# Attention by four heads: key chunks of 128, two half chunks sharing the array by quarters, and one weight load moved ahead

## Chip, cores and metric

The kernel runs on one core of a Trainium2 chip. The metric is the device time of one execution in microseconds, the median of the runs shown. The profile is of one further execution.

## The reference, cut to what matters

Three stages follow one another. Batch 4, 12 heads, 448 positions, 64 columns for each head:

```python
scores = scale * np.matmul(q, k.transpose(0, 1, 3, 2)) - np.log(S)     # q, k, v: (4, 12, 448, 64)
attn = 1.0 / (1.0 + np.exp(-scores))
attn_out = np.matmul(attn, v)
x = attn_out.transpose(0, 2, 1, 3).reshape(1792, 768)
h = np.maximum(np.maximum(x @ w1, x @ w2), x @ w3)                     # w1, w2, w3: (768, 768)
x2 = h @ w_out                                                        # (768, 768)
g, val = x2 @ w_gate, x2 @ w_val                                      # (768, 1536) each
out = (g / (1.0 + np.exp(-g)) * val) @ wo2                            # (1536, 768)
```

The sigmoid has no sum over the keys, so the keys may be taken in any order and in chunks of any size. Keys and values must only be cut in the same way.

## The kernel before, in words

**Number format.** A product that needs near float32 accuracy is made of three matmuls in a faster 32-bit format (`PRODUCTS`): high part by high part, low by high, high by low. The pair of parts is made by `halves` or `split`: a cast, then a subtraction. The second attention product (probabilities by values) uses plain float32 operands, and the trace shows two matmul instructions for each of its `nc.tensor.matmul` calls.

**Attention.** Heads come in pairs: 24 of them, six for each batch. `load_pair` brings q, k and v of a pair in by nine DMAs on SP's queue: four for `rq`, four for `rk` (runs of 32 values) and one for `rv`. VectorE transposes q and k by blocks of 32 into `qT` and `kT`, where the first head lies on partitions 0 to 63 and the second on 64 to 127, and `halves` makes `qq` and `kk`. The 448 keys are cut into four chunks of 112. `score(c)` makes six matmuls, three products by two heads, with 64 rows of the array for each head; ScalarE turns the two banks of `ps` into probabilities `a` (L759). `attend(c0, c1)` multiplies two chunks at a time by the values, 64 columns of the array for each head, and adds into one bank. `close` copies that bank out as the two parts of `x`, or to DRAM (`dx`) for the rows that are worked on later.

**The order of the work.** Nothing is written out by hand. Each step is a task with a cost for each engine that may do it, what it reads and writes, and a due time. `Plan.order` lists the tasks against its own model of time, and among those that can start soon takes the one due first. The result is a fixed order of instructions for each engine, SP's queue included. Due times come from constants: `HEAD` and `PAIR` are the time of one pair in the first and the second half of attention, `T0` is when the first layer's products begin, `AHEAD0` to `AHEAD2` spread the early conversion of `w_gate` and `w_val` (`ahead`), of which the first `NEAR` of 24 units go through the first set of buffers (`raw`) and the others through a second (`raw2`, one load at a time).

**Stages.** First attention alone, for batches 0 and 1. From `T0` on the 36 products of the first layer for the first 768 rows (18 matmuls of 384 columns each, `m<-x,w`) are interleaved with attention of batches 2 and 3. Then `w_out` for those rows (`second_layer`). Then the first layer for the other 1024 rows in seven products instead of eight (`first_layer_1`, `stream`, `mult`): it needs left factors made from the weights by `seven` and right factors made from `dx` by `x_back` and `right`. Each product takes terms of all three right factors. `seven` and `x_back` both fetch through the two buffers `cc`, in the order in which the program adds them: `x_back` 0, 1 and 2 with two buffers each, and then `seven`. After that come `w_out` for these rows and the gated part.

**Buffers.** In PSUM: `m` three banks, `av` one, `ps` two times two banks, later `mm` in place of `ps`. The attention of batches 0 and 1 accumulates in `m`, the rest in `av`. `S`, which `seven` needs, belongs to a region (`rest`) that opens only when the first layer's input `x` is done with.

Of the kernel before, what the change touches and what calls it, by code (L numbers as in the profile page):

```python
# [62 lines left out]

HEAD = 6000.0
T0 = 78.0 * 1000.0
PAIR = 5900.0
EARLY = 9000.0
LAG = 4500.0


NEAR = 18
AHEAD0 = 78.0 * 1000.0
AHEAD1 = 270.0 * 1000.0
# [152 lines left out]
def t_mm(n):  # L226
    return 13.3 + n / 2.4


def sigmoid_attention_max_ffn_silu_ffn(tc, q, k, v, w1, w2, w3, wo, wg, wv, wo2, out):  # L230
# [27 lines left out]
    P = 128  # L258
# [6 lines left out]
    NO = DM // 2  # L265
    KC = 4
    C = S // KC
    PARTS = ((0, 768), (768, B * S))
# [42 lines left out]
    def turn(old, new):  # L311
# [85 lines left out]
    N1 = 3 * KF * 2  # L397
    STEP = p_mm(0) + NPAIR * (B - 2) * PAIR / N1
    T1 = T0 + N1 * STEP

    def pair_at(b, p):
        i = b * NPAIR + p
        if b < 2:
            return i * HEAD, i * HEAD + LAG
        t = T0 + (i - 2 * NPAIR) * N1 * STEP / (NPAIR * (B - 2)) - EARLY
        return t, t + 1.5 * LAG
# [147 lines left out]
    def seven(s, w, i, keep=True):  # L554
# [20 lines left out]
        cc = fetch_pair(d, d.pieces)  # L575
        sb = rest.buf("S", [P, 4, HC])
        s2, s3, s1, s4 = (sb.part() for _ in range(4))
# [34 lines left out]
    def rows_pair(s, i):  # L612

        out_ = []
        for j in range(2):
            wb = two.buf("wr", [P, 2, UC], F32R)
            if not s:
# [7 lines left out]
                continue  # L625
            rt, sb = half.buf("cc", [P, 2, UC]), rest.buf("S", [P, 4, HC])
            low, c = sb.part(), sb.part()
# [54 lines left out]

    def load_pair(b, h0):
# [7 lines left out]
        rv = att.buf("rv", [C, 2, KC, D])  # L691
# [22 lines left out]
    def pair(b, p):  # L714

        due_s, due_a = pair_at(b, p)
        step = (HEAD if b < 2 else PAIR) / KC  # L720
        rq, rk, rv = load_pair(b, 2 * p)
        half = [slice(0, D), slice(D, P)]

        def operand(key, raw, name):
# [7 lines left out]
            both = att.buf(name, [P, 2, S], F32R)  # L732
            return both, halves(t, both, slice(0, S), lambda: t.t, S, key=name)

        qq, q_b = operand("qT", rq, "qq")
        kk, k_b = operand("kT", rk, "kk")
        probs, pav = [], None

        def score(c):
# [12 lines left out]
            t = plan.add(  # L752
                {"pe": 100.0 + 3 * t_mm(S)}, run, reads=[*q_b, *k_b], writes=[psb], after=prev("s"),
                due=due_s + c * step,
            )
            in_turn("s", t)
            plan.add(
                {"act": t_act(2 * S)},
                lambda e: e.activation(ab.t[:C], psb.t[:C, :, :S], AF.Sigmoid, bias=bias[:C], scale=SCALE),  # L759
                reads=[psb], writes=[ab], after=prev("a"),  # L760
            )
            in_turn("a", ab.writers[-1])
            probs.append(ab)

        def attend(c0, c1):

            nonlocal pav
            if c0 == 0:
                pav = pm.buf("av" if b > 1 else "m", [P, 512])
# [8 lines left out]
            t = plan.add(  # L778
                {"pe": 150.0 + (c1 - c0) * 4 * S / 2.4}, run, reads=[rv, *probs[c0:c1]], writes=[pav],
                after=prev("av"), due=due_a + c0 * step,  # L780
            )
            in_turn("av", t)

        def close():

            n = min(max(PARTS[0][1] - b * S, 0), S)
            if n:
# [23 lines left out]

        return score, attend, close

    def attention(b):
        for p in range(NPAIR):
            score, attend, close = pair(b, p)
            for c in range(KC):
                score(c)
            for c in range(0, KC, 2):
                attend(c, c + 2)  # L820
            close()

# [231 lines left out]

    def first_layer_1(facs):
        plan.kind = "b"
        hs = [None] * KF
        for i in range(HD):
# [5 lines left out]
            for wi, w in enumerate((w1, w2, w3)):  # L1064
# [117 lines left out]
    plan.kind = "h"  # L1182
    for b in range(B):
        attention(b)
    turn([att, ps], [pmb, half])
# [17 lines left out]
    hs = first_layer_1(facs)  # L1203
    plan.kind = "w"
# [41 lines left out]
```

## Time and profile before

| what | value |
|---|---|
| median of three runs | 992.12 us (991.72 to 997.26) |
| the profiled execution: its own time, its span | 992.58 us, 990.5 us |
| TensorE busy | 972.7 us, 98% of the span |
| VectorE, ScalarE, GpSimd busy | 641.9, 440.3, 141.8 us |
| granted TensorE clock, mean | 0.993 |

The span runs from the first to the last instruction; the time outside it is 2.1 us. A busy TensorE counts pipelined matmuls, so 98% says that it hardly waits, not that it computes at its peak.

### The profile page before, as it was taken

To read this page: it belongs to the slowest core of one execution; us is meant where nothing else is said; L and a number is where in the kernel's file an instruction comes from. 1 tells how busy PE (TensorE), PEld (TensorE's weight loads), DVE (VectorE), ACT (ScalarE), POOL (GpSimd) and SP (SyncE) were. 2 spreads that over 40 slices of the span, in tenths; PEclk is the share of its full clock that TensorE was granted. 3 is DMA by queue.
4 is the path that set the end of the run, shared out by engine and by line. 5 is a ranking of instruction groups with operands and counts; after the bars stand their busy time and mean duration, and the time that the engine had idled before them with its cause. 6 is when DMAs were issued, how large, how long until landed. Compare 5 with 4: busy or idle time off the path is not lost.

```text
span 990.5 us, 13658 instructions
## 1 busy us (share of the span) xinstructions
PE 972.7 (98%) x5139; PEld 816.0 (82%) x5139; DVE 641.9 (65%) x972; ACT 440.3 (44%) x618; POOL 141.8 (14%) x113
## 2 busy tenths in 40 slices
PE   8999999999999799999999999999999999999998
PEld 4444777777799688888878989898898999999998
DVE  5664576666667787874678486958687743455545
ACT  5876577677765643322445451605154322111110
POOL 0101000000000112320002022325344400000000
PEclk9999999999999899999999999999999999999999
DMA  7888999999989651125237665748589874567542
GB/s 125 185 170 184 246 291 274 259 292 252 306 303 309 233 160 49 64 74 181 92 125 278 240 230 184 271 167 271 192 304 321 282 262 175 184 215 244 184 143 100
DMA packets 191202, 208.52 MB, mean 211 GB/s; under 512 B 116128, under 2 KB 166560, under 8 KB 191136
## 3 DMA queue, kind: packets, MB, share of 16 engines
q1 hardware_dynamic: 191136, 207.65, 66.7%
q8 instruction: 40, 0.66, 0.3%
q14 instruction: 26, 0.21, 0.1%
HBM read 132.91 MB, written 74.71 MB: 210 GB/s over the span
## 4 chain that ended last, share of the span: by engine, by line
PE 87%; DMA 5%; DVE 3%; ACT 2%; SPq 2%; issue 1%; DVEq 0%; ACTq 0%
PE m L867 45%; PE mm L867 20%; PE av L867 12%; PE ps L747 5%; PE av L774 4%; DMA wraw<-in_moe_w_dram 2%; SPq L698 2%; PE m L774 1%; DMA wraw<-in_moe_w_val_dram 1%; DMA rq<-in_q_dram 1%; ACT a L759 1%; DVE u L665 1%; DMA cc<-dh 1%; DVE o L1151 0%; DVE w L349 0%
## 5 line engine op out<-in xcount | busy, mean ns | idle before, releaser
L867 PE MATMUL m<-T,w 128*128 128x512 f32 (+1 forms) x1557 | 334.0, 369 | 1.0 <-DVE T L349 0.9
L867 PEld LDWEIGHTS m<-T,w 128*128 128x128 f32 x1557 | 284.2, 188 | 40.5 <-DVE T L349 2.0
L867 PE MATMUL mm<-wr,g 128*128 128x384 f32 x1008 | 177.1, 334 | 0.1
L867 PEld LDWEIGHTS mm<-wr,g 128*128 128x128 f32 x1008 | 175.1, 188 | 0.9 <-DVE o L1151 0.4
L1023 DVE TENSOR_TENSOR u<-m,u 128x512 f32<-128x512 f32 (+1 forms) x111 | 71.2, 644 | 92.6 <-PE m L867 90.8
L867 PEld LDWEIGHTS m<-x,w 128*128 128x128 f32 x648 | 110.8, 188 | 20.1 <-issue 12.1
L867 PE MATMUL av<-T,w 128*128 128x512 f32 (+1 forms) x522 | 119.8, 373 | 6.4 <-ACT w L346 5.9
L867 PE MATMUL m<-x,w 128*128 128x384 f32 x648 | 122.0, 340 | 0.0
L867 PEld LDWEIGHTS av<-T,w 128*128 128x128 f32 x522 | 96.5, 190 | 20.5 <-ACT w L346 6.2
L1151 DVE TENSOR_TENSOR o<-mm,o 128x768 f32<-128x768 f32 (+1 forms) x84 | 67.8, 821 | 57.6 <-PE mm L867 57.6
L759 ACT ACTIVATE a<-ps,bias 112x896 f32<-112x896 f32 x96 | 91.5, 1004 | 11.4 <-PE ps L747 11.1
L747 PE MATMUL ps<-qq,kk 64*112 64x448 f32 x576 | 73.9, 385 | 5.0 <-ACT a L759 3.6
L747 PEld LDWEIGHTS ps<-qq,kk 64*112 64x112 f32 x576 | 47.0, 175 | 37.8 <-ACT a L759 21.1
L445 ACT ACTIVATE r<-wraw 128x768 int32<-128x768 uint32 x48 | 43.6, 908 | 54.3 <-DMA wraw<-in_moe_w_dram 16.2
L349 POOL TENSOR_TENSOR g<-t,g 128x512 fp32r<-128x512 f32 (+1 forms) x21 | 28.0, 1332 | 249.3 <-ACT g L346 240.1
L466 DVE SCALAR_TENSOR_TENSOR c<-c,r 128x768 int32<-128x768 int32 x48 | 46.2, 962 | 21.0 <-ACT r L458 16.1
L458 ACT ACTIVATE r<-wraw 128x768 f16<-128x768 f32 x48 | 52.1, 1086 | 0.9
L346 ACT CAST w<-S 128x768 fp32r<-128x768 f32 x34 | 28.5, 837 | 50.8 <-PE m L867 33.1
L346 ACT CAST g<-t 128x384 fp32r<-128x384 f32 (+1 forms) x43 | 23.9, 560 | 56.9 <-DVE t L1092 52.2
L583 POOL TENSOR_TENSOR S<-cc 128x384 f32<-128x384 f32 x16 | 16.9, 1057 | 196.6 <-DVE w L349 135.8
L867 PE MATMUL mm<-h,w 128*128 128x384 f32 (+1 forms) x216 | 44.2, 362 | 0.0
L774 PE MATMUL m<-a,rv 112*64 112x448 f32 x192 | 43.1, 571 | 0.0
(105 smaller groups left out, 1010.4 us busy)
## 6 DMA issues: line engine op xcount, KB each, us to landing
ds_S<-w SPq DMA_DIRECT2D x24, 768.0 KB, 4.4
w<-ds_S SPq DMA_DIRECT2D x24, 768.0 KB, 5.4
dp<-c SPq DMA_DIRECT2D x42, 384.0 KB, 6.1
cc<-dp SPq DMA_DIRECT2D x21, 768.0 KB, 5.1
wraw<-in_moe_w_dram SPq DMA_DIRECT2D x18, 768.0 KB, 6.2
wraw<-in_moe_w_gate_dram SPq DMA_DIRECT2D x12, 768.0 KB, 6.7
wraw<-in_moe_w_val_dram SPq DMA_DIRECT2D x12, 768.0 KB, 6.2
ds_A<-w SPq DMA_DIRECT2D x12, 768.0 KB, 6.4
```

Of the source, the lines that this page charges most:

```text
L346: (eng.copy if eng is nc.scalar else eng.tensor_copy)(o, i)
L349: eng.tensor_tensor(out=o, in0=a, in1=b, op=ALU.subtract)
L445: lambda e: e.activation(rb_at(), word(0).bitcast(U32), AF.Copy, scale=0.875 * 2.0 ** -29, bias=0.4999),
L458: lambda e: e.activation(rb_at().bitcast(F16).rearrange("p (c two) -> p c two", two=2)[:, :, 1], word(1).bitcast(F32), AF.Copy, scale=2.0 ...
L466: lambda e: e.scalar_tensor_tensor(c_at().bitcast(I32), c_at().bitcast(I32), 3, rb_at(), ALU.logical_shift_left, ALU.bitwise_or),
L698: nc.sync.dma_start(out=r.t[D * j + 32 * e:D * j + 32 * e + 32], in_=src[b, h0 + j, :, 32 * e:32 * e + 32].rearrange("(c i) d -> i c d", i ...
L747: nc.tensor.matmul(psb.t[:C, j, :S], kk.t[half[j], wh, c * C:(c + 1) * C], qq.t[half[j], xh], start=(i == 0), stop=(i == 2),)
L759: lambda e: e.activation(ab.t[:C], psb.t[:C, :, :S], AF.Sigmoid, bias=bias[:C], scale=SCALE),
L774: nc.tensor.matmul(pav.t[half[j], :S], rv.t[:, j, c], probs[c].t[:C, j], start=(c == 0), stop=(c == KC - 1),)
L867: nc.tensor.matmul(acc.at(n), l(), r(), start=(i == 0), stop=(i == len(terms) - 1))
L1023: lambda e: e.tensor_tensor(out=o.t[:, :n], in0=acc.at(n), in1=x.t[:, :n], op=ALU.add),
L1151: lambda e, o=o, b=banks[0].b, nh=nh: e.tensor_tensor(out=o.t[:, nh], in0=b.t[:, nh, :NO], in1=o.t[:, nh], op=ALU.add),
```

## The change

Attention goes by quads, two pairs of heads at a time. Of the 448 keys 384 are taken as three chunks of 128, and chunk `c` is now every third key from `c` on (so that a partition of `rv` reads three keys in one run of 768 bytes). The last 64 keys of both pairs make one common chunk: pair `g` takes the columns of half `g` of the array and head `j` the rows of half `j`, so four matmuls of 64 by 64 in plain float32 use the four quarters, from `kT` and `qT` themselves; the four matmuls by the values use the quarters too. A quad has seven score steps where two pairs had eight. Two steps together still make one `attend` task, which may now reach from one quad into the next (`group`, `flush`). `rv` comes by two DMAs instead of one. Attention always accumulates in `av`, which has two banks now, and `m` has two instead of three; later products alternate between `m` and `av`. The attention rings are longer. The constants of due times are others, with `SPREAD` putting the second half's attention into the first 0.8 of the interleaved stage, and `NEAR` falls from 18 to 12. `S` moves to the region `half`, which opens earlier, and the first `seven` is added after two of the three `x_back`.

```diff
-HEAD = 6000.0
-T0 = 78.0 * 1000.0
-PAIR = 5900.0
+QUAD = 10600.0
+T0 = 71.0 * 1000.0
+SPREAD = 0.8
...
-NEAR = 18
-AHEAD0 = 78.0 * 1000.0
+NEAR = 12
+AHEAD0 = 71.0 * 1000.0
...
-    KC = 4
-    C = S // KC
+    CW = S // P
+    KW = CW * P
+    KC = CW + 1
...
-        "att", dict(rq=2, rk=2, rv=3, qT=2, kT=2, qq=2, kk=2, a=4, xf=2), side="right",
+        "att", dict(rq=2, rk=2, rv=4, qT=3, kT=3, qq=3, kk=3, a=5, xf=2), side="right",
     )
-    half = Region("half", {"cc": 2, "u": 4, **{f"T0{i}": 1 for i in range(7)}}, side="right")
-    rest = Region("rest", {"S": 1, **{f"T{kk}{i}": 1 for kk in range(1, HD) for i in range(7)}}, side="right")
+    half = Region("half", {"cc": 2, "u": 4, "S": 1, **{f"T0{i}": 1 for i in range(7)}}, side="right")
+    rest = Region("rest", {f"T{kk}{i}": 1 for kk in range(1, HD) for i in range(7)}, side="right")
...
-    pm = Region("pm", dict(m=3, av=1), space=PSUM)
+    pm = Region("pm", dict(m=2, av=2), space=PSUM)
...
-        t = T0 + (i - 2 * NPAIR) * N1 * STEP / (NPAIR * (B - 2)) - EARLY
+        t = T0 + (i - NPAIR) * SPREAD * N1 * STEP / NPAIR - EARLY
...
+
             nc.sync.dma_start(
-                out=rv.t.rearrange("p h c d -> p (h c) d"),
-                in_=v[b, h0:h0 + 2].rearrange("h (c p) d -> p (h c) d", p=C),
+                out=rv.t[:, :, :CW], in_=v[b, h0:h0 + 2, :KW].rearrange("h (p c) d -> p h c d", c=CW),
+            )
+            nc.sync.dma_start(
+                out=rv.t[side, :, CW], in_=v[b, h0:h0 + 2, KW:].rearrange("h p d -> p h d"),
             )
...
             def run(_):
+                if len(gs) > 1:
+                    for g in gs:
+                        (qt, *_), (kt, *_), _ = pairs[g]
+                        for j in range(2):
+                            nc.tensor.matmul(
+                                psb.t[half_p[g], j, :S], kt.t[half_p[j], cols], qt.t[half_p[j]], start=True, stop=True,
+                            )
+                    return
+                (_, qq, _), (_, kk, _), _ = pairs[gs[0]]
                 for i, (xh, wh) in enumerate(PRODUCTS):
                     for j in range(2):
                         nc.tensor.matmul(
-                            psb.t[:C, j, :S], kk.t[half[j], wh, c * C:(c + 1) * C], qq.t[half[j], xh],
+                            psb.t[:, j, :S], kk.t[half_p[j], wh, cols], qq.t[half_p[j], xh],
                             start=(i == 0), stop=(i == 2),
                         )
...
             def run(_):
-                for c in range(c0, c1):
+                for g in gs:
+                    at = half_p[g] if len(gs) > 1 else slice(0, P)
                     for j in range(2):
                         nc.tensor.matmul(
-                            pav.t[half[j], :S], rv.t[:, j, c], probs[c].t[:C, j], start=(c == 0), stop=(c == KC - 1),
+                            accs[g].t[half_p[j], :S], pairs[g][2].t[at, j, c], ab.t[at, j],
+                            start=first[g], stop=last[g],
                         )
...
+        A, X, Z = (0,), (0, 1), (1,)
+        n = 0
+        for gs, c, first, last in (
+            *((A, c, {0: c == 0}, {0: False}) for c in range(CW)),
+            (X, CW, {0: False, 1: True}, {0: True, 1: False}),
+            *((Z, c, {1: False}, {1: c == CW - 1}) for c in range(CW)),
+        ):
+            ab = score(n, gs, slice(KW, S) if gs == X else slice(c, KW, CW))
+            attend(n, gs, c, ab, first, last)
+            ends.extend(lambda g=g: close(g) for g in gs if last[g])
+            n += 1
+            if len(group) == 2:
+                flush()
+        return flush
...
-        return Acc(pm.buf("av" if "late" in chain and count % 4 == 3 else "m", [P, 512]))
+        return Acc(pm.buf("av" if "late" in chain and count % 2 else "m", [P, 512]))
...
-                left = seven(1, w, i, keep=False)
+                if i or wi:
+                    left = seven(1, w, i, keep=False)
...
-    facs = [x_back(i) for i in range(HD)]
+    facs = [x_back(i) for i in range(2)]
+    plan.kind = "w"
+    left = seven(1, w1, 0, keep=False)
+    plan.kind = "x"
+    facs += [x_back(i) for i in range(2, HD)]
```

## Rows read from the trace of the kernel before

**Rows 1.** The page: the chain that ended last, shares of the span by engine.

```profile
PE 87%; DMA 5%; DVE 3%; ACT 2%; SPq 2%; issue 1%; DVEq 0%; ACTq 0%
```

**Rows 2.** Windows by stage: busy us and instructions per engine, granted clock, DMA share, GB/s.

```profile
7.80:94.20 86.40, 82.65 (x513) 38.17 (x513) 53.30 (x97) 65.05 (x83) 8.88 (x6) 0.96 0.85 171
94.20:276.70 182.50, 182.47 (x1063) 137.10 (x1061) 115.38 (x183) 126.00 (x152) 4.00 (x3) 1.00 0.95 272
276.70:320.40 43.70, 43.70 (x252) 43.55 (x252) 33.01 (x52) 27.15 (x44) 0.00 (x0) 1.00 0.89 302
320.40:331.30 10.90, 4.49 (x11) 3.01 (x11) 7.85 (x13) 6.92 (x10) 0.38 (x1) 0.69 0.93 322
331.30:453.70 122.40, 122.40 (x541) 101.35 (x541) 96.33 (x136) 44.12 (x62) 28.68 (x25) 1.00 0.33 106
```

**Rows 3.** Timeline of TensorE in attention alone: start, length (us), line, count.

```profile
56.37 1.46 PE L747 MATMUL ps<-qq,kk 64*112 64x448 f32 x12
57.76 1.72 PE L774 MATMUL m<-a,rv 112*64 112x448 f32 x8
59.41 0.46 PE L747 MATMUL ps<-qq,kk 64*112 64x448 f32 x2
```

**Rows 4.** Score matmuls and weight loads, 56.2 to 59.5 us: shortest, median, longest (ns).

```profile
L747 PEld LDWEIGHTS ps<-qq,kk x14: 169/171/173, 56.4 to 59.4; 64*112 64x112 f32 x14
```

**Rows 5.** The chain in order of time: start, length (us), what.

```profile
110.31 3.33 PE m L867 x18
...
289.37 6.24 PE m L867 x36
...
331.29 6.12 PE m L867 x27
```

**Rows 6.** Groups by form: count, busy us, mean ns, idle before and its releasers.

```profile
L466 DVE SCALAR_TENSOR_TENSOR c<-c,r 128x768 int32<-128x768 int32 x48 | 46.2, 962 | 21.0 <-ACT r L458 16.1 <-ACT c L451 4.4
L452 DVE TENSOR_SCALAR c<-wraw 128x768 f32<-128x768 f32 x37 | 20.9, 564 | 30.8 <-DMA dp<-c 23.0 <-DMA wraw<-in_moe_w_dram 3.9 <-DMA wraw<-in_moe_w_out_dram 2.7
L346 DVE CAST w<-c 128x768 fp32r<-128x768 f32 x19 | 10.6, 557 | 0.4
```

**Rows 7.** Timeline of TensorE where the first layer's second part begins.

```profile
326.50 1.22 PE L867 MATMUL av<-T,w 128*128 128x512 f32 x2 [5.92 <-ACT w L346]
```

**Rows 8.** The fetches into `cc` on SP's queue there, and ScalarE's first split.

```profile
303.67 0.32 SPq L831 DMA_DIRECT2D cc<-dx  x1
...
311.42 0.32 SPq L831 DMA_DIRECT2D cc<-dx  x1
...
318.54 0.60 SPq L538 DMA_DIRECT2D cc<-dp  x1
...
325.61 0.83 ACT L346 CAST w<-cc 128x768 fp32r<-128x768 f32 x1 [0.37 <-DMA cc<-dp]
```

**Rows 9.** One fetch each, issued at 318.54, 4.30 and 4.84 us: KB, us to landing.

```profile
cc<-dp SPq DMA_DIRECT2D x1, 768.0 KB, 7.1
...
rk<-in_k_dram SPq DMA_DIRECT2D x1, 56.0 KB, 2.1
...
rv<-in_v_dram SPq DMA_DIRECT2D x1, 224.0 KB, 3.8
```

**Rows 10.** Timeline of SP's queue in attention alone: start, time of issue (us), count.

```profile
53.39 2.07 SPq L698 DMA_DIRECT2D rq<-in_q_dram  x4
...
71.42 0.49 SPq L706 DMA_DIRECT2D rv<-in_v_dram  x1
72.00 5.50 SPq L698 DMA_DIRECT2D rq<-in_q_dram  x4
```

**Rows 11.** Timeline, 72 to 80 us: the twelfth pair's last transpose and its scores.

```profile
72.25 0.65 DVE L728 STREAM_TRANSPOSE kT<-rk 128x448 f32<-128x448 f32 x1 [0.32 <-DMA rk<-in_k_dram]
...
74.71 1.50 PE L747 MATMUL ps<-qq,kk 64*112 64x448 f32 x12
...
79.74 1.76 PE L747 MATMUL ps<-qq,kk 64*112 64x448 f32 x12 [1.87 <-ACT a L759]
```

More of the change, by code (lines that the diff above doesn't have):

```diff
@@ L397, in sigmoid_attention_max_ffn_silu_ffn, with quad_at @@
     N1 = 3 * KF * 2
-    STEP = p_mm(0) + NPAIR * (B - 2) * PAIR / N1
+    STEP = p_mm(0) + NPAIR * (B - 2) * QUAD / 2 / N1
     T1 = T0 + N1 * STEP
-    def pair_at(b, p):
-        i = b * NPAIR + p
+    def quad_at(b, g):
+        i = b * (NPAIR // 2) + g
         if b < 2:
-            return i * HEAD, i * HEAD + LAG
-        t = T0 + (i - 2 * NPAIR) * N1 * STEP / (NPAIR * (B - 2)) - EARLY
+            return i * QUAD, i * QUAD + LAG
+        t = T0 + (i - NPAIR) * SPREAD * N1 * STEP / NPAIR - EARLY
         return t, t + 1.5 * LAG
@@ L575, in seven @@
         cc = fetch_pair(d, d.pieces)
-        sb = rest.buf("S", [P, 4, HC])
+        sb = half.buf("S", [P, 4, HC])
         s2, s3, s1, s4 = (sb.part() for _ in range(4))
@@ L625, in rows_pair @@
                 continue
-            rt, sb = half.buf("cc", [P, 2, UC]), rest.buf("S", [P, 4, HC])
+            rt, sb = half.buf("cc", [P, 2, UC]), half.buf("S", [P, 4, HC])
             low, c = sb.part(), sb.part()
@@ L681, in sigmoid_attention_max_ffn_silu_ffn, with load_pair @@
     dram_x = {}
-    def load_pair(b, h0):
+    def load_pair(b, h0, side):
         def fetch(dst, cost, run):
@@ L690, in load_pair @@
         rq, rk = (att.buf(key, [P, NB, 32]) for key in ("rq", "rk"))
-        rv = att.buf("rv", [C, 2, KC, D])
+        rv = att.buf("rv", [P, 2, KC, D])
         for src, r in ((q, rq), (k, rk)):
@@ L712, in load_pair, with quad @@
         return rq, rk, rv
[L714 to L722, printed above, removed]
+    half_p = [slice(0, D), slice(D, P)]
+    group = []
+    def quad(b, p0):
+        due_s, due_a = quad_at(b, p0 // 2)
+        step = QUAD / 7
         def operand(key, raw, name):
@@ L732, in operand, with score @@
             both = att.buf(name, [P, 2, S], F32R)
[L733 to L739, printed above, removed]
+            return t, both, halves(t, both, slice(0, S), lambda: t.t, S, key=name)
+        pairs = []
+        for g in range(2):
+            rq, rk, rv = load_pair(b, 2 * (p0 + g), half_p[g])
+            pairs.append((operand("qT", rq, "qq"), operand("kT", rk, "kk"), rv))
+        accs = [None, None]
+        def score(n, gs, cols):
             psb = ps.buf("ps", [P, 2, 512])
@@ L752, in score @@
             t = plan.add(
-                {"pe": 100.0 + 3 * t_mm(S)}, run, reads=[*q_b, *k_b], writes=[psb], after=prev("s"),
-                due=due_s + c * step,
+                {"pe": 100.0 + (3 * t_mm(S) if len(gs) == 1 else 4 * S / 2.4)}, run,
+                reads=[x for g in gs for y in pairs[g][:2] for x in (y[2] if len(gs) == 1 else y[:1])],
+                writes=[psb], after=prev("s"), due=due_s + n * step,
             )
@@ L758, in score @@
                 {"act": t_act(2 * S)},
-                lambda e: e.activation(ab.t[:C], psb.t[:C, :, :S], AF.Sigmoid, bias=bias[:C], scale=SCALE),
+                lambda e: e.activation(ab.t, psb.t[:, :, :S], AF.Sigmoid, bias=bias, scale=SCALE),
                 reads=[psb], writes=[ab], after=prev("a"),
@@ L762, in score, with attend, flush, close @@
             in_turn("a", ab.writers[-1])
[L763 to L769, printed above, removed]
+            return ab
+        def attend(n, gs, c, ab, first, last):
+            for g in gs:
+                if first[g]:
+                    accs[g] = pm.buf("av", [P, 512])
             def run(_):
-                for c in range(c0, c1):
+                for g in gs:
+                    at = half_p[g] if len(gs) > 1 else slice(0, P)
                     for j in range(2):
                         nc.tensor.matmul(
-                            pav.t[half[j], :S], rv.t[:, j, c], probs[c].t[:C, j], start=(c == 0), stop=(c == KC - 1),
-                        )
+                            accs[g].t[half_p[j], :S], pairs[g][2].t[at, j, c], ab.t[at, j],
+                            start=first[g], stop=last[g],
+                        )
+            group.append((run, [*(pairs[g][2] for g in gs), ab], [accs[g] for g in gs], due_a + n * step))
+        def flush():
+            todo, group[:] = list(group), []
             t = plan.add(
-                {"pe": 150.0 + (c1 - c0) * 4 * S / 2.4}, run, reads=[rv, *probs[c0:c1]], writes=[pav],
-                after=prev("av"), due=due_a + c0 * step,
+                {"pe": 150.0 + len(todo) * 4 * S / 2.4}, lambda e: [run(e) for run, *_ in todo],
+                reads=[x for _, r, _, _ in todo for x in r], writes=[x for _, _, w, _ in todo for x in w],
+                after=prev("av"), due=todo[0][3],
             )
             in_turn("av", t)
-        def close():
+            for f in ends:
+                f()
+            ends[:] = []
+        def close(g):
+            p, pav = p0 + g, accs[g]
             n = min(max(PARTS[0][1] - b * S, 0), S)
@@ L810, in close, with attention @@
             plan.add({"sp": 650.0}, store, reads=[xf], writes=[piece], tail=TAIL, due=due_a + 20000.0)
[L812 to L821, printed above, removed]
+        A, X, Z = (0,), (0, 1), (1,)
[12 more added lines that the diff above has]
+        return flush
+    ends = []
+    def attention():
+        for b in range(B):
+            for p0 in range(0, NPAIR, 2):
+                flush = quad(b, p0)
+        if group:
+            flush()
     def x_back(i):
@@ L1053, in stream, with first_layer_1 @@
         last(0, 1, mult("S4", "B22"), u[1])
-    def first_layer_1(facs):
+    def first_layer_1(facs, left):
         plan.kind = "b"
@@ L1182, in sigmoid_attention_max_ffn_silu_ffn @@
     plan.kind = "h"
-    for b in range(B):
-        attention(b)
+    attention()
     turn([att, ps], [pmb, half])
@@ L1202, in sigmoid_attention_max_ffn_silu_ffn @@
         ahead(w, f, False, AHEAD1 + (i + 1) * (AHEAD2 - AHEAD1) / (len(todo) - NEAR), raw2, AHEAD1)
-    hs = first_layer_1(facs)
+    hs = first_layer_1(facs, left)
     plan.kind = "w"
```

## The prediction

> **What bounds the kernel now.** I read the chain of waits first. It lies 87% on TensorE [rows 1], so a microsecond taken from TensorE counts unless something else becomes late, and only there. Then I cut the span into stages by windows [rows 2]. In attention alone, 7.8 to 94.2 us, TensorE is busy 82.65 of 86.40 us with a mean clock of 0.96. From there to 320.4 us it never rests. Then comes the one large hole, 320.4 to 331.3 us: 4.49 of 10.90 us busy and a mean clock of 0.69. The next stage is full again. So the change touches three places: attention alone, attention among products, and the hole.
>
> The reader should also see the transfers. The DMA share is 0.85, 0.95, 0.89 and 0.93 in the first four windows and 0.33 in the fifth [rows 2]. The loads are nearly as tight as TensorE as far as 331 us, and slack behind it.
>
> **Attention on TensorE.** A block is two chunks. Its twelve score matmuls start at 56.37 us, its eight value matmuls at 57.76, the next block at 59.41 [rows 3]: 1.39 + 1.65 = 3.04 us. Two chunks for 24 pairs are 48 blocks now. The change makes 12 quads of seven steps, 84 steps or 42 blocks: 6 x 3.04 = 18.2 us less, half of it in each half of attention. That chunks have 128 keys and not 112 adds nothing to a matmul that streams the same 448 columns.
>
> The common chunk costs some of it back. Its score is plain float32, in the two-instruction form of the value matmuls, where one chunk takes 1.65/2 = 0.83 us; an ordinary chunk's score takes 1.39/2 = 0.70: +0.13. It also changes how the array is divided, once more among the scores and once more among the values. What such a change costs I read from the products: 18 matmuls alone between others take 3.33 us, 36 in a row 6.24, so 3.12 for 18 [rows 5]: 0.21 each. So +0.13 + 2 x 0.21 = 0.55 for each quad, 6.6 us for 12. No row shows the array in four quarters. The bounds are no extra (18.2 us gained) and twice as many changes (another 5.0 us lost); I take the middle, since rows 3 show halves by rows and halves by columns each running their two matmuls together. Net: -18.2 + 6.6 = -11.6 us.
>
> [...]
>
> **Weights with a step.** The score's key columns now lie three elements apart. A weight load of 112 columns lasts 171 ns [rows 4], and its matmuls follow every 1.39/6 = 0.23 us; 128 columns would take 171 x 128/112 = 195 ns and stay hidden. The nearest rows for reading with a step are on VectorE: every second word of 768 takes 564 ns, a cast of 768 neighbours 557 [rows 6]. So I take zero; the other bound is a rival below.
>
> **Products of the first layer.** Before, almost each of the 36 stands between attention blocks and pays the 0.21. With attention pressed into 0.8 of the stage, the last seven or so follow one another: 7 x 0.21 = -1.5 us (bounds 0 and -3). Three banks of `m` become two. The cover is the next product: a bank is needed again over 3 us after it was filled, and an eviction takes about half a microsecond. Zero; if an eviction waits behind a conversion that itself waits for a load, it costs one wait at a time.
>
> **Loads in attention alone.** SP issues four DMAs for q in 2.07 us [rows 10], 0.52 each. A pair had nine and gets ten, 5.2 us instead of 4.7: over 12 pairs +6.2 us on a queue whose values of the twelfth pair went out at 71.42 us. [...] The values go in longer runs. At the start one `rk` DMA landed 2.1 us after its issue at 4.30 us and the `rv` behind it 3.8 us after 4.84, so `rv` took 8.64 - 6.40 = 2.2 us of the transfers [rows 9]; runs three times as long may save between 0 and 1.4 us of it, I take 0.6, 7 us for 12 pairs. So the queue's end moves little, perhaps 1.5 us earlier, while TensorE's work there shrinks by 6. Before, the twelfth pair's last transpose began at 72.25 us and its scores at 74.71 [rows 11], some 2.5 us of slack. 6 - 1.5 - 2.5 = 2 us of new waiting: +2 (bounds 0 and +5). Behind an SP that is late stand the first weights and the stores of `dx`; with `T0` at 71 they are not pressing. The wait of 1.87 us at 79.74 [rows 11], a probability step behind a conversion, can go or turn up elsewhere; I leave it, plus or minus 2.
>
> **The hole at 320 us.** Nine matmuls of 512 columns take 6.12/3 = 2.04 us [rows 5]. Here they took the window's 10.90, so 8.9 us were lost: 5.92 of standing still until ScalarE's split of a left factor [rows 7], and most of the rest in matmuls at the lower of the two clock levels after the rest. The split ran at 325.61 when the fetch landed; the fetch was issued at 318.54, behind `x_back`'s at 303.67 and 311.42 [rows 8], and took 7.1 us to land [rows 9]. The change gives `seven` the place of 303.67 or so, and moves the last two fetches of `x_back` back by one place each. The left factors then are early. But the second product needs a difference of both halves of the third right factor: if that fetch goes out at 318.5 and takes 7.1 us, it lands at 325.6, and the hole is only some 2 us shorter. [...] I take -5 (bounds 0 and -8.9).
>
> **Six units moved.** They go to where the DMA share is 0.33 and VectorE busy 96.33 of 122.40 us [rows 2]. Each adds 0.96 + 0.56 us on VectorE [rows 6], 9 us in all: 105 of 122. Covered, zero. Were VectorE late, the products would wait for banks.
>
> **Sum.** On the profiled execution, span 990.5: -11.6 - 1.5 + 2 - 5 = -16.1, so 974.4 us; with 2.1 outside the span 976.5. That execution lies 0.5 us above the median (992.58 against 992.12): **976.0 us**.
>
> **Rivals.**
> First: the hole stays, as a wait for the right factor instead of the left one, and the loads hold attention back in full. Then 5 and 3 us of the sum fail: 984. For it speaks that SP's queue and `cc` keep their two buffers and their order; against it, the lighter traffic.
>
> Second, the change doesn't do what it says: quarters of the array do not run four at a time but two. Then the common chunk takes double its 0.83 us in scores and again in values, 1.66 a quad, 20 us in 12: 996. For it: in the trace matmuls only ever run in twos. Against: both kinds of two are there, by rows and by columns.
>
> Third, slower than before: reading weights with a step of three slows their loads. It decides once a load lasts longer than the 0.23 us between matmuls. At half pace 195 becomes 390 ns, 0.16 more for each pair of matmuls; 12 quads x 6 chunks x 3 pairs = 216, so +35 us: 1011. For it: nothing in the trace reads with so wide a step. Against: VectorE's step of two, which costs 7 ns in 557. [...]
>
> **How the numbers follow.** Forecast, all terms inside their bounds: 0.58. First rival 0.22. Second 0.08. Third 0.07. Better than every middle value, near 960: 0.05. For the range I add the terms' bounds as independent misses: about 8 to 9 us either way from 976, and the first rival's 984 with the same again halved. 963 to 989 holds the forecast and most of the first rival, and leaves out the second, the third and the extreme. A change of about 1% is what this measurement can tell, the runs before lying between 991.72 and 997.26. Below 982.2 us lie the forecast but for its upper end (0.53), a third of the first rival (0.08) and the best case (0.05): faster 0.66. Above 1002.0 lies the third rival and a piece of the second: slower 0.09. Within 1%: 0.25.
>
> **What the profile after would show.** Blocks of 3.04 us seven for two quads, with the common chunk's four score matmuls of 64 by 64 starting together in 0.8 us; if they start in twos, the second rival. Score weight loads near 195 ns with matmuls 0.2 us apart; near 390 the third. The first value blocks of the last batches end earlier by some 6 us when `m<-x,w` begins and by 13 when it ends. In the hole, ScalarE's split ahead of the last product of `second_layer`, and TensorE waiting, if at all, for VectorE's `T` or `u`. VectorE no longer idle between 331 and 454 us but TensorE still full. The prediction is wrong if SP's queue, not TensorE, carries the chain before 80 us, or if the hole is as long as before.

## The result and the profile after

| | before | after |
|---|---|---|
| median, beside each other on one chip | 994.38 us (991.72 to 997.26, 4 runs) | 980.85 us (978.36 to 981.55, 4 runs) |
| ratio after to before | | 0.9859 [0.9819, 0.9899] |
| profiled execution, span | 992.58, 990.5 us | 978.36, 976.1 us |

The forecast was 976.0 us (963 to 989), with a span 16.1 us shorter; the span is 14.4 us shorter. The place of the gain is not quite the forecast one. The chain of waits of the kernel after, shares of the span:

```profile
PE 82%; DMA 7%; DVE 4%; SPq 3%; issue 2%; ACT 1%; DVEq 0%; ACTq 0%
```

TensorE's share falls from 87% [rows 1], and DMA with SP's queue rises from 7% to 10%: the chain now runs through loads somewhere. In the first 80 us TensorE has 8.1 + 5.5 + 2.2 = 15.8% of it (10.7 + 10.3 = 21.0% in the kernel before). The chain of the kernel after by line, from 0 to 80 us, as far as the view prints it:

```profile
by line: SPq L699 29.2%; DMA rk<-in_k_dram 18.5%; PE av L793 8.1%; issue 6.1%; DMA rq<-in_q_dram 5.9%; DVE kT L734 5.7%; PE ps L764 5.5%; DVE kk L347 3.3%; SPq L711 2.4%; DVE kk L350 2.4%; PE ps L757 2.2%; DVE x L350 1.8%; SPq L708 1.8%; DV
```

The windows say where TensorE loses time. After, columns as in [rows 2]:

```profile
50.80:60.10 9.30, 6.22 (x26) 1.97 (x24) 5.48 (x10) 4.81 (x6) 0.00 (x0) 0.63 0.71 132
53.90:60.04 6.14, 6.14 (x22) 1.90 (x22) 4.05 (x8) 3.28 (x4) 0.00 (x0) 0.52 0.71 131
315.40:331.30 15.90, 15.90 (x71) 13.13 (x71) 14.27 (x21) 9.75 (x15) 2.32 (x2) 1.00 0.89 300
331.30:443.90 112.60, 112.60 (x498) 93.23 (x498) 97.09 (x138) 51.96 (x71) 29.95 (x25) 1.00 0.53 173
```

One stretch in attention alone, 50.8 to 60.1 us, is bad: 3.08 us standing, and the 6.14 us behind it at a mean granted clock of 0.52: 0.50 in each microsecond from 53.9 to 58.9, and 1.00 again from 59.9. (The 0.63 of the whole window counts the standing too.) The lower clock costs 6.14 x 0.48 = 2.9, so the stretch loses 6.0 us. The hole of before (4.49 of 10.90 us busy at 0.69; the clock stood at 0.50 from 326.4 to 330.0 us) is gone: from 315.40 to 331.30 us TensorE is busy throughout and the clock is 1.00.

Two points of the chain split the gain. `w_out` for the first rows began before at

```profile
283.13 6.24 PE mm L867 x36
```

and the second product after it at 331.29 [rows 5]. After, the chain in order of time (start, length, what):

```profile
277.79 6.39 PE mm L910 x36
...
317.47 2.04 PE m L910 x9
```

| piece of the span | forecast | measured |
|---|---|---|
| until `w_out` begins (attention, products, loads) | -11.1 | 277.79 - 283.13 = -5.3 |
| from there to the second product of the next stage (the hole) | -5 | 39.68 - 48.16 = -8.5 |
| the rest | 0 | 658.6 - 659.2 = -0.6 |

So the first piece gave half of what was forecast and the hole gave more. Attention after, timeline of TensorE:

```profile
18.73 1.56 PE L764 MATMUL ps<-qq,kk 64*128 64x448 f32 x12
20.23 1.72 PE L793 MATMUL av<-a,rv 128*64 128x448 f32 x8
21.88 1.56 PE L764 MATMUL ps<-qq,kk 64*128 64x448 f32 x12
...
53.90 1.77 PE L757 MATMUL ps<-qT,kT 64*64 64x448 f32 x8 [3.08 <-ACT a L777]
...
61.54 1.89 PE L793 MATMUL av<-a,rv 64*64 64x448 f32 x12
63.35 1.56 PE L764 MATMUL ps<-qq,kk 64*128 64x448 f32 x12
...
66.50 0.95 PE L764 MATMUL ps<-qq,kk 64*128 64x448 f32 x6
67.38 0.98 PE L757 MATMUL ps<-qT,kT 64*64 64x448 f32 x8
68.29 1.72 PE L793 MATMUL av<-a,rv 128*64 128x448 f32 x8
...
245.91 31.88 PE L910 MATMUL m<-x,w 128*128 128x384 f32 x180
```

Read from start to start, an ordinary block is 1.50 + 1.65 = 3.15 us (3.04 before). The common chunk's eight score instructions take 68.29 - 67.38 = 0.91 us, about what an ordinary chunk takes: the four quarters run side by side. The pair of score chunks with the common one takes 68.29 - 66.50 = 1.79 against 1.50, its values 63.35 - 61.54 = 1.81 against 1.65: +0.45 us for each quad.

That holds where both pairs are ready. In three common chunks of attention alone the second pair's matmuls start only when the first pair's are through, and TensorE's rows count that as busy. Timeline of its weight loads, the second pair's in two of them; the first pair's start at 25.03 and 42.70:

```profile
25.93 0.20 PEld L757 LDWEIGHTS ps<-qT,kT 64*64 64x64 f32 x4 [0.71 <-DVE kT L734]
...
43.55 0.19 PEld L793 LDWEIGHTS av<-a,rv 64*64 64x64 f32 x4 [0.66 <-DVE x L350]
```

The one waited for the second pair's `kT`, the other for VectorE's copy out of the accumulator bank. With a third one, at 30.86 us, 0.90 + 0.85 + 1.06 = 2.8 us are lost so.

Who was late at 53.90? The row names a probability step `a`. VectorE and ScalarE just before it:

```profile
51.70 0.65 DVE L734 STREAM_TRANSPOSE qT<-rq 128x448 f32<-128x448 f32 x1 [1.90 <-DMA rq<-in_q_dram]
52.37 0.56 ACT L347 CAST qq<-qT 128x448 fp32r<-128x448 f32 x1 [4.96 <-DVE qT L734]
52.84 1.90 ACT L777 ACTIVATE a<-ps,bias 128x896 f32<-128x896 f32 x2
```

ScalarE's order has a cast of a later pair's `qT` ahead of two probability steps that had their scores. The cast waits 4.96 us for the transpose, the transpose for the load of `rq`, and TensorE finds both banks of `ps` unread. SP's queue there (start, time of issue):

```profile
41.27 2.97 SPq L699 DMA_DIRECT2D rq<-in_q_dram  x4
...
46.43 0.42 SPq L708 DMA_DIRECT2D rv<-in_v_dram  x1
46.90 0.61 SPq L711 DMA_DIRECT2D rv<-in_v_dram  x1
47.60 2.12 SPq L699 DMA_DIRECT2D rq<-in_q_dram  x4
...
51.91 0.42 SPq L708 DMA_DIRECT2D rv<-in_v_dram  x1
...
71.48 0.42 SPq L708 DMA_DIRECT2D rv<-in_v_dram  x1
```

The late `rq` went out from 47.60 us. SP issues almost without a gap: one pair takes 51.91 - 46.43 = 5.48 us. Half a quad on TensorE is (3.5 x 3.15 + 0.45) / 2 = 5.7. SP is hardly quicker, and any hold-up of the queue (2.97 us for four, at 41.27) stays.

### The profile page after: what moved, and what is told of

Read it like the earlier page. It is cut to its first block, busy times and chain, and to the rows that moved or that the text cites. A ratio compares the mean times of both kernels' runs of the same rounds, so it can differ in the third digit from the quotient of the medians.

```text
span 976.1 us, 13549 instructions
## 1 busy us (share of the span) xinstructions
PE 962.9 (99%) x5091; PEld 814.1 (83%) x5091; DVE 642.6 (66%) x968; ACT 431.5 (44%) x608; POOL 145.7 (15%) x115
## 4 chain that ended last, share of the span: by engine, by line
PE 82%; DMA 7%; DVE 4%; SPq 3%; issue 2%; ACT 1%; DVEq 0%; ACTq 0%
PE m L910 30%; PE av L910 23%; PE mm L910 22%; PE av L793 3%; SPq L699 3%; PE ps L764 3%; DMA rk<-in_k_dram 2%; DMA wraw<-in_moe_w_out_dram 1%; DMA rq<-in_q_dram 1%; DMA wraw<-in_moe_w_dram 1%; DMA wraw<-in_moe_w_val_dram 1%; DVE kT L734 1%; DMA wraw<-in_moe_w_gate_dram 1%; DMA rv<-in_v_dram 1%; PE ps L757 1%
## 5 line engine op out<-in xcount | busy, mean ns | idle before, releaser
L910 PE MATMUL av<-T,w 128*128 128x512 f32 (+1 forms) x1044 | 235.8, 369 | 0.7 <-DVE T L350 0.7
L910 PE MATMUL m<-T,w 128*128 128x512 f32 (+1 forms) x1035 | 233.1, 369 | 0.0
L910 PEld LDWEIGHTS av<-T,w 128*128 128x128 f32 x1044 | 190.9, 188 | 26.8 <-DVE T L350 1.1
L910 PEld LDWEIGHTS m<-T,w 128*128 128x128 f32 x1035 | 189.5, 188 | 25.7
L1066 DVE TENSOR_TENSOR u<-m,u 128x512 f32<-128x512 f32 (+1 forms) x75 | 48.0, 644 | 72.0 <-PE m L910 71.7
L777 ACT ACTIVATE a<-ps,bias 128x896 f32<-128x896 f32 x84 | 80.9, 1003 | 24.6 <-PE ps L764 19.9
L793 PE MATMUL av<-a,rv 128*64 128x448 f32 (+1 forms) x384 | 77.8, 563 | 0.1
L764 PEld LDWEIGHTS ps<-qq,kk 64*128 64x128 f32 x432 | 46.1, 254 | 32.4 <-ACT a L777 16.9
L446 ACT ACTIVATE r<-wraw 128x768 int32<-128x768 uint32 x48 | 43.7, 909 | 53.3 <-DMA wraw<-in_moe_w_gate_dram 15.8
L764 PE MATMUL ps<-qq,kk 64*128 64x448 f32 x432 | 62.5, 414 | 3.7 <-ACT kk L347 2.5
L1066 DVE TENSOR_TENSOR u<-av,u 128x512 f32<-128x512 f32 (+1 forms) x72 | 45.9, 641 | 21.5 <-PE av L910 21.3
```

The source lines that it names most:

```text
L446: lambda e: e.activation(rb_at(), word(0).bitcast(U32), AF.Copy, scale=0.875 * 2.0 ** -29, bias=0.4999),
L764: nc.tensor.matmul(psb.t[:, j, :S], kk.t[half_p[j], wh, cols], qq.t[half_p[j], xh], start=(i == 0), stop=(i == 2),)
L777: lambda e: e.activation(ab.t, psb.t[:, :, :S], AF.Sigmoid, bias=bias, scale=SCALE),
L793: nc.tensor.matmul(accs[g].t[half_p[j], :S], pairs[g][2].t[at, j, c], ab.t[at, j], start=first[g], stop=last[g],)
L910: nc.tensor.matmul(acc.at(n), l(), r(), start=(i == 0), stop=(i == len(terms) - 1))
L1066: lambda e: e.tensor_tensor(out=o.t[:, :n], in0=acc.at(n), in1=x.t[:, :n], op=ALU.add),
```

## The experiments

The first four kernels of the table, then the next four, then the last four ran together, each group on one chip beside the kernel before (medians 995.3, 994.5 and 994.09 us). "`w_out` begins" is the first `mm<-h,w` in the timeline of the profiled execution; the kernel before has 282.97 there, after 277.63.

| run | median us | ratio to before | `w_out` begins |
|---|---|---|---|
| left_only | 996.90 | 1.0021 [1.0001, 1.0041] | 285.16 |
| left_late | 981.47 | 0.9860 [0.9826, 0.9895] | 280.69 |
| rests_apart | 994.60 | 0.9995 [0.9980, 1.0009] | 292.45 |
| contig | 979.59 | 0.9842 [0.9814, 0.9870] | 278.78 |
| near12_before | 1001.19 | 1.0069 [1.0046, 1.0091] | 289.87 |
| near18 | 990.11 | 0.9950 [0.9919, 0.9981] | 279.08 |
| pool_values | 970.45 | 0.9751 [0.9710, 0.9792] | 271.78 |
| more_issues | 986.81 | 0.9917 [0.9890, 0.9945] | 286.55 |
| spread1 | 979.60 | 0.9858 [0.9832, 0.9884] | 276.96 |
| before_pool | 991.27 | 0.9970 [0.9952, 0.9988] | 283.70 |
| pool_late | 968.49 | 0.9756 [0.9725, 0.9787] | 267.03 |
| pool_late_near | 967.27 | 0.9737 [0.9712, 0.9763] | 266.83 |

### left_only: the earlier left factor alone, on the kernel before

```diff
-    facs = [x_back(i) for i in range(HD)]
+    facs = [x_back(i) for i in range(2)]
+    left = seven(1, w1, 0, keep=False)
+    facs += [x_back(i) for i in range(2, HD)]
```

with `S` in `half`, as in the change.

> The kernel before with only the earlier left factors (S in the earlier region, the first seven after two x_back). If the late left factor alone made the hole of 8.9 us at 320 us: about 8 to 9 us under the kernel before, a ratio near 0.991, and TensorE full from 310 to 335 us. Rival, the third right factor becomes the late one since its two fetches move back: 2 to 3 us under it, ratio 0.997, and a hole of 6 to 7 us that ends at VectorE's T or u.

No gain. Timeline of TensorE of left_only:

```profile
329.31 1.54 PE L867 MATMUL m<-T,w 128*128 128x512 f32 x6
336.33 0.80 PE L867 MATMUL m<-T,w 128*128 128x512 f32 x1 [5.48 <-ACT T L346]
```

The left factor `w` is in time, and the wait of 5.92 us [rows 7] comes back as 5.48 for `T`, the right factor, one product later. That is the first rival's mechanism, on the old order of work. Of the two cases expected it is the second, but without its 2 to 3 us of gain.

### left_late: the change with the left factor where it was

The same edit taken back in the kernel after.

> The changed kernel with the left factors as late as before, all else changed. If the early fetch fills the hole: 8 to 9 us over the changed kernel, about 989 us, ratio to the kernel before 0.995, hole back at about 315 us. Rival, the lighter transfer queue (12 early conversions for 18) fills it: 981 to 985 us, ratio 0.987 to 0.991, hole of 0 to 4 us.

Nothing is lost, against 8 to 9 us expected of the main case. Timeline of TensorE of left_late, the first two products behind `w_out`:

```profile
318.13 2.24 PE L910 MATMUL av<-T,w 128*128 128x512 f32 x9
320.21 2.20 PE L910 MATMUL m<-T,w 128*128 128x512 f32 x9
```

No wait is left at either factor. The change of place is neither enough (left_only) nor needed (left_late).

### rests_apart: the 64 remaining keys of each pair in a chunk of their own

```diff
-            (X, CW, {0: False, 1: True}, {0: True, 1: False}),
...
+            *((A, c, {0: c == 0}, {0: c == CW}) for c in range(KC)),
+            *((Z, c, {1: c == 0}, {1: c == CW}) for c in range(KC)),
```

Eight steps in a quad; the rest's chunk uses half the rows. `QUAD` is 12.0 and `T0` 78 us to suit.

> The changed kernel with the rests of 64 keys of the two pairs in chunks of their own, half the array each: 96 score steps and not 84, QUAD 12000 and T0 78000 as the longer work wants. If TensorE's time in attention sets the time everywhere: 6 blocks of 3.1 us more, less the 6 us that the common chunks cost, so 10 to 13 us over the changed kernel, about 993 us, ratio 0.998. Rival, the loads set the first half: only the second half's share, 4 to 7 us more, about 986 us, ratio 0.992, and TensorE waits less in the first 80 us than the changed kernel does.

The gain is gone: 994.60 - 980.85 = 13.8 us more, and all of it lies ahead of `w_out`. Timeline of TensorE of rests_apart:

```profile
292.45 6.40 PE L909 MATMUL mm<-h,w 128*128 128x384 f32 x36
```

This is 14.8 us later than after (277.63), as its profiled execution is 14.8 longer (993.17 against 978.36). By the blocks of the kernel after the 12 steps are worth 6 x 3.15 - 12 x 0.45 = 13.5 us, close to it. The changed due times are in the measured figure too, and so are the extra changes of division that a rest's chunk of its own brings (0.21 us each by the prediction's estimate [rows 5]), so the agreement is not exact.

### contig: the step of three taken out of the weights

```diff
-            ab = score(n, gs, slice(KW, S) if gs == X else slice(c, KW, CW))
+            ab = score(n, gs, slice(KW, S) if gs == X else slice(c * P, (c + 1) * P))
```

Scores and values then belong to different keys, so only its time is read.

> The changed kernel with chunk c made of 128 neighbouring keys in the scores, so that the weights have no step; the values are as they were, so scores and values of different keys are multiplied and only the time can be read. If the step slows the weight loads: loads near 195 ns instead of 249, a block of twelve score matmuls 1.42 us instead of 1.49, 2 to 3 us less in all, ratio to before 0.983. Rival, the loads are hidden and the longer block comes from 128 columns for 112: loads 195 to 249, block 1.47 to 1.49, no change, ratio 0.986.

Weight loads of a tile (shortest, median, longest in ns), after and then contig:

```profile
L764 PEld LDWEIGHTS ps<-qq,kk x102: 247/248/261, 16.0 to 48.6; 64*128 64x128 f32 x102
```

```profile
L764 PEld LDWEIGHTS ps<-qq,kk x102: 182/184/188, 15.9 to 47.6; 64*128 64x128 f32 x102
```

Timeline of TensorE of contig:

```profile
28.23 1.48 PE L764 MATMUL ps<-qq,kk 64*128 64x448 f32 x12
29.64 0.59 PE L793 MATMUL av<-a,rv 64*64 64x448 f32 x2
```

With the step a load takes 248 ns instead of 184, and twelve score matmuls 1.50 us instead of 1.41. That is 42 x 0.09 = 3.8 us by the blocks; the medians differ by 1.3 and their intervals overlap. Windows from the first score to `w_out`, after and then contig, show where the rest went:

```profile
8.45:277.63 269.18, 264.61 (x1560) 180.76 (x1561) 174.77 (x285) 177.47 (x220) 15.06 (x10) 0.98 0.85 226
```

```profile
8.21:278.78 270.57, 261.62 (x1560) 172.80 (x1561) 175.54 (x285) 176.96 (x220) 15.07 (x10) 0.98 0.84 224
```

TensorE is busy 3.0 us less and stands 8.95 us instead of 4.57. So the step costs TensorE 3 to 4 us of work, and taking it out alone saves hardly any time here: the waits grow by at least as much.

### near12_before and near18: the number of early conversions, on either kernel

`NEAR` 18 to 12 in the kernel before, and 12 to 18 in the kernel after.

> The kernel before with 12 early conversions in the first part instead of 18, nothing else. If the queue of transfers made the hole at 320 us: the fetch for the left factors lands in 4 to 5 us instead of 7, the hole of 8.9 us shrinks to 0 to 2, ratio to before 0.991 to 0.993. Rival, the hole went with the new order of the interleaved stage (T0, QUAD, SPREAD): hole as before, ratio 1.000.

> The changed kernel with 18 early conversions in the first part again. If the queue made the hole: a hole of 4 to 9 us at about 315 us, 985 to 990 us, ratio to before 0.990 to 0.995; the early left factor may save part of it, but then the wait is for the right factor. Rival, the new order did it: no hole, 981 us, ratio 0.986.

The kernel before gets 6.7 us slower, where a gain was expected. Its hole is larger, and in the profiled execution `w_out` begins 6.9 us later, in a planned order that is another too. Timeline of TensorE of near12_before, then of near18:

```profile
335.15 1.22 PE L867 MATMUL av<-T,w 128*128 128x512 f32 x2 [7.67 <-ACT w L346]
```

```profile
318.60 1.52 PE L910 MATMUL m<-T,w 128*128 128x512 f32 x6
322.92 0.50 PE L910 MATMUL m<-T,w 128*128 128x512 f32 x1 [2.80 <-ACT T L347]
324.05 1.22 PE L910 MATMUL m<-T,w 128*128 128x512 f32 x2 [0.62 <-DVE T L350]
...
328.07 2.23 PE L910 MATMUL m<-T,w 128*128 128x512 f32 x9
```

In the kernel after, 18 early conversions bring 2.80 + 0.62 = 3.42 us of standing back, at the right factor. From 318.60 to 328.07 us stand 18 matmuls, which take 4.08 us at the full clock, so 9.47 - 4.08 = 5.4 us are lost, 2.0 of them beyond the standing; the mean granted clock of 0.88 from 318 to 332 us accounts for 14 x 0.12 = 1.7 of these. Its `w_out` begins 1.5 us later than after's, and its profiled execution is 6.7 us above that of after, about the sum of the two; the median is 9.3 above, and no trace shows the rest. So in the kernel after the smaller number is needed for closing the hole; on the old order of the stage before it, it doesn't close it.

### spread1: attention of the second half spread over the whole interleaved stage

`SPREAD` 0.8 to 1.0 in the kernel after.

> The changed kernel with SPREAD 1.0: attention of batches 2 and 3 due over the whole interleaved stage instead of its first 0.8. The fetch buffers cc open only when attention is over (245 us in the changed kernel, 276 in the one before). If that early opening removed the hole: a hole of 5 to 9 us at about 315 us again, 985 to 990 us, ratio to before 0.991 to 0.995. Rival, the hole went by the changed mix of conversions alone: no hole, 981 to 983 us, ratio 0.986 to 0.988.

Attention ends at about 264 us, not 246, and still no hole follows. Timeline of TensorE of spread1:

```profile
317.33 2.20 PE L910 MATMUL m<-T,w 128*128 128x512 f32 x9
```

The theory that an early end of attention starts the fetches early, and so closes the hole, falls.

What goes with the hole is when the last fetch of the right factors goes out. SP's queue of left_only, near18, spread1 and after:

```profile
329.65 0.32 SPq L831 DMA_DIRECT2D cc<-dx  x1
```

```profile
315.68 0.32 SPq L874 DMA_DIRECT2D cc<-dx  x1
```

```profile
311.65 0.32 SPq L874 DMA_DIRECT2D cc<-dx  x1
```

```profile
309.74 0.32 SPq L874 DMA_DIRECT2D cc<-dx  x1
```

That is 0.3 us behind the start of the second product in left_only, and 2.9, 5.7 and 7.7 us ahead of it in the others. The first two wait at the right factor, 5.48 and 2.80 us; the last two don't.

### pool_values and more_issues: SP's queue in attention alone

pool_values issues both DMAs of `rv` from GpSimd; more_issues cuts the first of them by head, so that SP issues eleven for each pair.

```diff
-            nc.sync.dma_start(
+            nc.gpsimd.dma_start(
```

```diff
+            for j in range(2):
+                nc.sync.dma_start(
+                    out=rv.t[:, j, :CW], in_=v[b, h0 + j, :KW].rearrange("(p c) d -> p c d", c=CW),
+                )
```

> The changed kernel with both transfers of the values issued by GpSimd instead of SP, in the same planned order. If SP's issuing sets the pace of attention alone (5.5 us a pair, ten issues): about 1.1 us less a pair, the stall of 3 us and the slow clock after it at 51 us gone, 3 to 6 us less, 975 to 978 us, ratio to before 0.980 to 0.983. Rival, TensorE's own blocks and the evictions set it: 980 to 981 us, ratio 0.986; a further case, GpSimd's issuing is late behind its other work, 983 us or more.

> The changed kernel with the first transfer of the values cut in two, one for each head, so that a pair has eleven issues on SP and the same bytes and runs. If SP's issuing sets the pace of attention alone: 0.52 us for each of 12 pairs, 4 to 7 us more, 985 to 988 us, ratio to before 0.990 to 0.993. Rival, SP has slack: 981 us, ratio 0.986.

One more issue for each pair costs 986.81 - 980.85 = 6.0 us, as expected (the intervals of the two ratios just overlap); SP's period of a pair grows to 5.94 us (after: 5.48). SP's queue in more_issues:

```profile
50.80 2.10 SPq L699 DMA_DIRECT2D rq<-in_q_dram  x4
...
56.74 2.10 SPq L699 DMA_DIRECT2D rq<-in_q_dram  x4
```

Two fewer gain 10.4, where 3 to 6 were expected. Windows of pool_values over the stretch that was bad:

```profile
50.80:60.10 9.30, 9.30 (x66) 4.47 (x64) 5.75 (x12) 6.67 (x10) 2.67 (x4) 1.00 1.01 165
```

TensorE is full at clock 1.00, although the DMA share is higher (1.01 against 0.71): the issuing queue held the loads up, not the transfers. The chain of pool_values in the first 80 us lies on TensorE for 38.8 + 34.3 + 7.0 + 4.2 = 84.3%:

```profile
by line: PE av L793 38.8%; PE ps L764 34.3%; PE ps L757 7.0%; DMA rk<-in_k_dram 5.9%; PE m L910 4.2%; SPq L699 4.1%; ACT a L777 2.5%; issue 0.9%; DVE kT L734 0.8%; ACT kk L347 0.7%; DVEq L734 0.1%; ACTq L777 0.0%
```

In the profiled executions `w_out` begins 5.9 us earlier and the end is 5.9 earlier (972.44 against 978.36). The bad stretch gives its 6.0 us back, and no common chunk runs pair after pair any more. The remaining 4.5 of the medians lie in which execution was profiled: after's is its fastest, 2.5 under the median, and pool_values' its slowest, 2.0 above. It also loses 2.0 us at the start, where after has its first scores at 8.45 us. First scores of pool_values:

```profile
10.46 4.08 PE L764 MATMUL ps<-qq,kk 64*128 64x448 f32 x18 [3.85 <-ACT kk L347]
```

### before_pool: the same queue in the kernel before

Its one DMA for `rv` issued from GpSimd.

> The kernel before with its one transfer of the values per pair issued by GpSimd instead of SP. If SP's issuing held the first half already: 2 to 5 us less, ratio to before 0.995 to 0.998. Rival, with nine issues per pair and TensorE's longer work SP had slack: no change, ratio 1.000, so the change itself made SP the limit.

A gain of 2.8 us, 0.997 [0.9952, 0.9988]; its profiled execution (993.34) shows none of it, so where it lies stays open. In that execution TensorE never stands from the first score to the first product, as it did before [rows 2], so SP's queue had a part in the old waits too; but among the products 3.8 us of standing come up. One issue of nine taken off SP is worth 2.8 us in the old kernel, two of ten are worth 10.4 in the new one, whose TensorE work is shorter.

### pool_late and pool_late_near: what can be put together

pool_late is pool_values with the first four pairs' values left on SP, and the second accumulator of a quad in batches 0 and 1 taken from `m`. pool_late_near has neighbouring keys in a chunk besides, in scores and values alike, at the price of a third DMA for `rv` in shorter runs.

```diff
+            q_v = nc.sync if b == 0 and h0 < 8 else nc.gpsimd
...
-                    accs[g] = pm.buf("av", [P, 512])
+                    accs[g] = pm.buf("m" if b < 2 and g else "av", [P, 512])
...
-            ab = score(n, gs, slice(KW, S) if gs == X else slice(c, KW, CW))
+            ab = score(n, gs, slice(KW, S) if gs == X else slice(c * P, (c + 1) * P))
```

> The changed kernel with the values of the first four pairs issued by SP and the others by GpSimd, and the second accumulator of batches 0 and 1 in the ring m. If four early values transfers made the first scores start 2 us later in the run with all on GpSimd: first scores at about 8.5 us, no wait for an accumulator, 967 to 969 us, ratio to before 0.973. Rival, the time is set by the later order: 970 us, ratio 0.975.

> The same with chunks of 128 neighbouring keys in scores and values, values in runs of 256 bytes, two transfers for the full chunks of a pair. If the step in the weights is the cost (0.08 us in each block of score matmuls): 3 us less than its partner, 964 to 966 us, ratio 0.970. Rival, the shorter runs slow the loads by as much or more: 968 to 975 us, ratio 0.973 to 0.980.

The late start is mended: pool_late's first scores come at 8.30 us. Timeline of TensorE of pool_late_near:

```profile
57.98 1.49 PE L766 MATMUL ps<-qq,kk 64*128 64x448 f32 x12
...
61.05 0.87 PE L766 MATMUL ps<-qq,kk 64*128 64x448 f32 x6
```

A block is 61.05 - 57.98 = 3.07 us. pool_late_near is the best version, 967.27 us and 0.9737 of before, faster than both kernels; from pool_late (968.49) it is not told apart, 1.2 us where 3 were expected of the step (up to `w_out` TensorE is busy 3.1 us less and stands 3.5 us more), and the two edits of pool_late were not run singly.

## Why the prediction held, point by point

**Attention on TensorE (forecast -11.6).** Six blocks are saved as said, and 42 blocks last 3.15 instead of 3.04 us: -18.2 + 42 x 0.11 = -13.6. The common chunk costs 0.45 x 12 = 5.4 (forecast 6.6). So -8.2. The term at fault is "weights with a step", which was put at zero: the loads take 248 ns, not 195, and contig brings the block's scores back to 1.41 us, against 1.39 with chunks of 112. (A block's eight value matmuls take 1.65 us with 112 keys [rows 3] and with 128.) The row chosen for it, VectorE's step of two, said nothing of TensorE's weight loads.

**First rival.** Half of it came: the loads held attention back in full, by about 5 us (below). Its wait for the right factor shows in left_only and near18, not in the kernel after.

**Third rival.** The rows settle it against the 1011: 248 ns is over the 0.23 between matmuls, its point of decision, yet matmuls of the two heads, on different rows of the array, still start every 1.50 / 6 = 0.25 us for a pair. Its mechanism is there, at 3 to 5 of its 35 us. The half pace that makes the 35 us no run shows: the step lengthens a load from 184 to 248 ns, by a third.

**Second rival.** Out: eight instructions in four quarters take 0.91 us, where two at a time would have needed 1.66; the chunks that ran pair after pair waited for an operand or a bank.

**Products in a row (-1.5).** Attention is over at 245.9 us and the last ten products take 31.9 up to `w_out`, 3.19 each against 3.33 between blocks: about -1.4, as forecast.

**Loads in attention alone (+2, bounds 0 to +5).** Mis-sized, at the outer bound. SP's 5.48 us for a pair is near the 5.2 forecast, and the twelfth pair's values go out at 71.48 us, as before at 71.42 [rows 10]; forecast was 1.5 us earlier. The 0.6 us a pair that longer runs were to save on the transfers is the author's estimate; no run shows it, and it could not help where issuing was the limit. (What held the four issues of 5.50 us [rows 10], no run shows either.) What TensorE loses to it needs both kernels. Up to `w_out` after stands 4.57 us (269.18 - 264.61) and loses about 69.60 x 0.07 = 4.9 at the lower clock and the 2.8 of the common chunks, 12.3 in all, 6.0 of them around the one stall:

```profile
8.40:78.00 69.60, 66.14 (x395) 31.36 (x395) 42.46 (x79) 42.71 (x52) 2.28 (x2) 0.93 0.68 126
```

Before lost 3.75 + 86.40 x 0.04 = 7.2 in attention alone [rows 2] and next to nothing behind it. So about +5.1, and the first scores come 0.6 us later (8.45 against 7.85). The wait was expected at TensorE's own operands; the longest came through ScalarE's order, as the 1.87 us at 79.74 [rows 11] had. more_issues (+6.0) and pool_values (-10.4) show the queue as the cause from both sides. In sum -8.2 - 1.4 + 5.1 + 0.6 = -3.9 against -5.3 measured; the last 1.4 us stay open.

**The hole (-5, bounds 0 to -8.9).** It gave -8.5, nearly all, and for another reason. The step that failed is that the left factors, once early, make the hole shorter: left_only shows that the move alone carries the wait over to the right factor (5.48 us for 5.92), left_late that it isn't needed. The 5 us, between the 2 that a landing at 325.6 us would have given and the bound of 8.9, no run shows: the move alone gained nothing, the whole change 8.5. The six early conversions fewer are needed in the kernel after, by near18, but near12_before shows no gain from them on the old order. near18's shorter hole lost clock too, about 2 us beyond its 2.80 + 0.62 of standing. What closes the hole is that the last fetch goes out in time, 5.7 and 7.7 us ahead of the second product in spread1 and after; which part of the new order (quads, longer rings, other PSUM banks) brings that stays open. It isn't the spread of attention alone, nor the common chunk or `T0` at 71: rests_apart has neither, and TensorE goes from `w_out` into its second product at 331.97 us without a wait.

**Six units moved (0).** Held: 331.30 to 443.90 us is full, VectorE 97.09 of 112.60.

So the span is right within 2 us by luck: two misses of opposite sign, +5.8 us ahead of `w_out` and -3.5 in the hole, cancel in part. (The median misses by 4.9, since after's profiled execution lies 2.5 us under its median.) One mark that the prediction set for being wrong was met: before 80 us the chain lies on SP's queue and the loads, and only 15.8% of it on TensorE. It was a weak mark, for the kernel before has no more than 21.0% there. The number held; the account of attention alone and of the hole did not.

## What to carry to other kernels

When TensorE's work in a stage is shortened, divide the issuing queue's time by the same unit of work: here 5.48 us a pair against 5.7 left no room, and two DMAs on another queue were worth 10 us. The late load hurt here through what stood behind its conversion in ScalarE's order (the cast waited 4.96 us, TensorE 3.08), so look there and not only at its consumer. A group of matmuls that counts as busy can hide a wait between its parts, 0.85 to 1.06 us here, so compare its length with that of its like. Moving one late transfer forward in a shared queue can make the next one late, as in left_only (a wait of 5.48 us for one of 5.92); try the move alone before counting its gain.

## What the runs showed of the hardware beyond that

Reading float32 weights three elements apart costs a load of 128 columns 248 ns instead of 184. The DMA engines stood at a share of 0.71 while loads were late, and at 1.01 in pool_values, with TensorE full: ten issues of 0.42 to 0.61 us each, 5.48 us a pair, and not the bytes, set the pace. Behind 3.08 us of standing still the mean granted clock was 0.52 for 6.14 us, so the stall cost 6.0 us, nearly twice its length.
